# Retention attention with a routed mixture of experts on one core: the gate arithmetic moved away from in front of the token counts

## The chip, the cores and the metric

The kernel is one program on one core of a Trainium2 chip. The metric is the device time of one execution in microseconds, less is better. A profiled execution of the kernel before the change is shown beside its timed runs.

## The reference

A retention attention (a linear attention with a decay per head) over 4 sequences of 768 tokens with 8 heads of 64 gives a matrix `x` of 3072 tokens by 512. Each token then goes to one of eight experts, and its result is weighted by a gate:

```
state = gamma * state + k_t v_t^T ;  y_t = scale * q_t state
x = y laid out as (3072, 512)
logits = x @ w_gate ;  e_idx = argmax(logits) ;  probs = softmax(logits)
gate_w = probs[n, e_idx] ;  eom = 1 / (1 + exp(-(x @ w_output_gate)))
for e in 0..7:  rows of expert e:
    out = gate_w * eom[:, e] * (relu(x @ w1[e]) @ w2[e])
```

## The kernel before

The work has three stages.

**Attention.** The 3072 tokens are 24 chunks of 128, `i` from 0 to 23, and one pass of the loop does one chunk. The order of PE (TensorE), DVE (VectorE), ACT (ScalarE) and POOL (GpSimd) is the order in which the code is written. In a chunk PE makes the scores `s` (L331), starts the output `py` from the state (L348), transposes the next chunk's keys into `pk` and queries into `pq` (L286, L304), transposes finished rows of an earlier chunk into `px` (`tokens`, L453), adds the masked scores to `py` (L353), and updates the state `st` (L361). DVE masks the scores into `am` (L335) and scales `py` into `yt` (L369). ACT copies `pk` to `kt` (L288) and `px`, times the gate, to a `row` (L506). The tiles `pk`, `pq` and `px` take turns in two PSUM buffers (pool `ps_t`, tag `t`), so `px` takes the buffer that `pk` had, and it can start only when ACT has copied `pk` out.

**Routing, in pairs of chunks.** For pair `n`, the even chunk computes the logits in the PSUM tile `misc` (L379, `route1`), and at its end `route1b` and `out_gate`. The odd chunk that follows computes the gate and the place of each token:

- `gates` (L467, L468): sum of the exponentials and the small constant. `gates_b` (L475, L477): the product with the output gate's denominator, and the reciprocal `gate`.
- `count` (L460, L461): two small matmuls that count, per expert, the tokens ahead of each token. They write columns 0 to 15 of the same `misc` tile in which `gates` and `gates_b` read and write other columns, and they are ordered with every earlier access to that tile.
- `route2` (L484 to L496): the row number `posi` of each token in the sorted buffer `srt` in DRAM.
- `build_row` and `scatter` (L506, L513): the finished rows, sent to `srt` by an indirect DMA from POOL.

Chunk 11 also ranks the experts by the counts so far, and chunk 19 (`EARLY`) looks whether the first expert has 256 rows.

**The head.** The 256 first rows of the likeliest expert are loaded from `srt` at chunk 21 (L577), split into two parts on ACT and POOL in chunk 22 (`head_prep`, L590 to L594), and multiplied by that expert's weights. These 192 matmuls (L603, L621) are a generator, and `run_head(n)` issues the next `n` of them, to fill holes of PE: `HB` of them in chunk 23, `H1`, `H2` and `H3` in the routing of the last pair, 24 behind it, and the rest after a branch on `n_low` (L781, L782), the number of experts with few tokens, which every engine reads. Their results go out through eight indirect DMAs of 128 rows of 128 numbers (L185, `ot`, `idx`).

Behind the last counts `totals` (L547, L549, L550) computes the tokens per expert. The last two rows are scattered, and SP loads the sorted rows of the first expert as soon as these scatters have landed (L832, `xl`), then the weights of the second expert, then the second expert's rows.

**Experts.** Eight experts of 8 steps each: `stage1` (L867) gives `h`, ACT and DVE split it into `hh` and `hl` (L871, L872), `stage2` (L885) of a step needs both and is issued behind the next step's `stage1`. `prep_x` (L848 to L855: `idi`, `xt`, `xh`, `xw`) prepares the next expert's rows, and `split_weights` (L176 to L181) its weights. In this stage the order on ACT, DVE and SP is set by a scheduler, that on PE and POOL by the code.

Of the kernel before, what the change touches and what calls it, by code (L numbers as in the profile page):

```python
# [32 lines left out]
def retention_moe_kernel(  # L33
# [159 lines left out]
    with ExitStack() as actx:  # L193
# [118 lines left out]
        yts, rt = {}, {}  # L312
# [72 lines left out]
        def small(name, *shape, dt=F32, bufs=2):  # L385
            return sm.tile([P, *shape], dt, name=name, tag=name, bufs=bufs)
# [42 lines left out]
        def route1b(n):  # L429
            oh, _, wm, acc = rt["r", n]  # L430
            lg, wk = rt.pop(("l", n))
            zk = in_psum(n, 128, 2, E)
            nc.vector.tensor_tensor(out=zk, in0=lg[:, :, E:2 * E], in1=oh, op=ALU.mult)
            z = small("z", 2)
            nc.vector.tensor_reduce(out=z, in_=zk, axis=AX.X, op=ALU.add)
            rt["z", n] = z

            nxt = small("acc", 2, E, dt=BF16)
            nc.vector.scalar_tensor_tensor(out=nxt[:, 0], in0=wk[:, 1], scalar=wm[:, 1:2], in1=acc[:, 1],
                                           op0=ALU.is_equal, op1=ALU.add)  # L440
            rt["acc"] = nxt

        def out_gate(n):
            ez = small("ez", 2)
            nc.scalar.activation(ez, rt.pop(("z", n)), AF.Exp, scale=-1.0)
            rt["ez", n] = ez
# [9 lines left out]
        def count(n):  # L456

            oh, acc = rt["r", n][0], rt["r", n][3]
            cnt = rt["misc", n][:, 0:2 * E]
            nc.tensor.matmul(cnt, tri_b, oh.rearrange("p c e -> p (c e)"), start=True, stop=False)  # L460
            nc.tensor.matmul(cnt, ones_b, acc.rearrange("p c e -> p (c e)"), start=False, stop=True)  # L461

        def gates(n):
            _, ex, wm, _ = rt["r", n]

            se = in_psum(n, 160, 2)
            nc.vector.tensor_reduce(out=se, in_=ex, axis=AX.X, op=ALU.add)  # L467
            nc.vector.tensor_scalar(out=se, in0=se, scalar1=1e-9, scalar2=None, op0=ALU.add)  # L468
            rt["se", n] = se

        def gates_b(n):
            wm = rt["r", n][2]
            se, ez = rt.pop(("se", n)), rt.pop(("ez", n))
            den = in_psum(n, 162, 2)
            nc.vector.scalar_tensor_tensor(out=den, in0=ez, scalar=1.0, in1=se, op0=ALU.add, op1=ALU.mult)  # L475
            gate = small("gate", 2)
            nc.vector.reciprocal(gate, den)  # L477
            rt["gate", n] = (gate, wm)

        def route2(n):  # L480
            oh, _, wm, _ = rt.pop(("r", n))
            cnt = rt["misc", n][:, 0:2 * E].rearrange("p (c e) -> p c e", c=2)
            rk = in_psum(n, 164, 2, E)
            nc.vector.tensor_tensor(out=rk, in0=cnt, in1=oh, op=ALU.mult)  # L484
            rank = in_psum(n, 180, 2)
            nc.vector.tensor_reduce(out=rank, in_=rk, axis=AX.X, op=ALU.add)

            ok = in_psum(n, 182, 2, E)
            nc.vector.tensor_scalar(out=ok, in0=cnt, scalar1=float(SLOTS), scalar2=None, op0=ALU.max)
            ov = small("ov", 2)  # L490
            nc.vector.tensor_reduce(out=ov, in_=ok, axis=AX.X, op=ALU.add)
            slot = small("slot", 2)
            nc.vector.scalar_tensor_tensor(out=slot, in0=wm, scalar=-float(SLOTS), in1=rank, op0=ALU.mult, op1=ALU.add)
            nc.vector.scalar_tensor_tensor(out=rank, in0=rank, scalar=float(SLOTS), in1=ov, op0=ALU.is_ge, op1=ALU.mult)
            posi = small("posi", 2, dt=I32, bufs=5)
            nc.vector.scalar_tensor_tensor(out=posi, in0=slot, scalar=float(E * SLOTS), in1=rank, op0=ALU.add, op1=ALU.max)  # L496
            rt["posi", n] = posi
# [68 lines left out]
        EARLY = 8  # L566
        LOAD0 = 2 * EARLY + 5
        backlog = []
        HB, H1, H2, H3 = 12, 8, 5, 4


        hd = {}
# [67 lines left out]
        def run_head(n):  # L640
            for _ in range(n):
                next(head, None)
# [17 lines left out]
        for i in range(NCH):  # L660
            b, c = divmod(i, NC)
            if i == LOAD0:

                n_late = nc.values_load(late[0:1, 0:1], min_val=0, max_val=1)
                with tc.If(n_late > 0):
                    fill(base0, cnt0, 0, HEAD, sm)
                head_load()
            if i + 3 < NCH:
                load_k(i + 3)
                load_v(i + 3)  # L670
            if i % 2 == 0 and i // 2 + 3 < B * NQ:
                load_q(i // 2 + 3)
            if 1 <= i < NC:
                more_gq(i)
            for e in clear_at.get(i, ()):
                clear(e)
            if i in w_at:
                load_weights(w_at[i])
            if i + 2 < NCH:
                prep_v(i + 2)  # L680

            n1 = i // 2 - 1 if i % 2 == 0 else -1
            n2 = i // 2 - 1 if i % 2 == 1 else -1

            def between():
                if n1 >= 0:
                    logits(n1)
                if i + 1 < NCH:
                    kt_block(i + 1)
                if i == 1:  # L690
                    spread_gates()
                if 0 < i and i + 2 < NCH:
                    qt_block(i + 2)
                if i == NCH - 1:
                    run_head(HB)
                if n1 >= 0:
                    route1(n1)
                if n2 >= 0:
                    gates(n2)
                    gates_b(n2)  # L700
                    count(n2)
                    misc = rt["misc", n2]
                    if n2 == PICK:
                        rank(totals(misc, rt["acc"][:, 0]), io8, pick)
                        nc.vector.tensor_copy(base0, pick[:, 0:1])
                        nc.vector.tensor_scalar(out=first, in0=io8, scalar1=base0, scalar2=None, op0=ALU.is_equal)
                        nc.vector.tensor_scalar(out=base0, in0=base0, scalar1=float(SLOTS), scalar2=None, op0=ALU.mult)
                        rank_e[0] = nc.values_load(pick[0:1, 0:1], engines=(mybir.EngineType.SP,), min_val=0, max_val=E - 1)
                    if n2 == EARLY:
                        tot = totals(misc, rt["acc"][:, 0])  # L710
                        cj = sm.tile([P, E], F32, name="cj", tag="cj")
                        nc.vector.scalar_tensor_tensor(out=cj, in0=tot, scalar=1.0, in1=first, op0=ALU.mult, op1=ALU.mult,
                                                       accum_out=cnt0)
                        nc.vector.tensor_scalar(out=late, in0=cnt0, scalar1=float(HEAD), scalar2=None, op0=ALU.is_lt)
                if i >= 3:
                    tokens(i - 3)
                if i == NCH - 1:
                    tokens(i - 2)
            def before_state():
                if i == 0:  # L720
                    qr_block(2)
                    qt_block(2)
                if n2 >= 0:
                    route2(n2)
                if i >= 3:
                    build_row(i - 3)
                if i + 3 < NCH:
                    qr_block(i + 3)

            attend(i, between, before_state)  # L730
            if n1 >= 0:
                route1b(n1)
                out_gate(n1)
            if i == NCH - 1:
                build_row(i - 2)
                break
            if i == LOAD0 + 1:
                head_prep()
            if i == LOAD0 - 1:
                flush(len(backlog))  # L740
            elif i == LOAD0:
                flush(len(backlog))
            elif i >= first_scatter:
                flush(2)
            for z in range(2):
                if i - 2 - z in w_at:
                    split_weights(w_at[i - 2 - z] + z)
# [4 lines left out]
        n = NCH // 2 - 1  # L752
# [5 lines left out]
            tokens(2 * n + c2, pl[:, c2])  # L758
        run_head(H3)
        count(n)  # L760
        route1b(n)
        out_gate(n)
        gates(n)
        gates_b(n)
        tot = totals(rt["misc", n], rt["r", n][3][:, 1], rt["r", n][0][:, 1])
        route2(n)
        for c2 in range(2):
            build_row(2 * n + c2)
# [7 lines left out]
        for j, n in enumerate((FILL, FILL - P)):  # L776
            nc.vector.tensor_scalar(out=lw, in0=cnts, scalar1=float(n), scalar2=None, op0=ALU.is_lt)
            nc.vector.tensor_reduce(out=no, in_=lw, axis=AX.X, op=ALU.add)
            nc.vector.tensor_copy(n_low[:, j:j + 1], no)
        run_head(24)  # L780
        n_few = nc.values_load(n_low[0:1, 0:1], min_val=0, max_val=E)  # L781
        with tc.If(n_few > 0):  # L782
            for e in range(E):
# [311 lines left out]
```

## Time and profile before

| What | Value |
|---|---|
| Time of the kernel before, median of 3 runs | 462.39 us (461.76 to 464.07) |
| Profiled execution, its own time | 463.1 us |
| Profiled execution, its span | 461.4 us |
| PE matmul busy | 434.5 us (94%) |
| DVE busy | 252.0 us (55%) |
| ACT busy | 191.3 us (41%) |
| POOL busy | 185.8 us (40%) |
| Mean granted TensorE clock | 0.973 |

Busy time is the sum of an engine's instructions. Matmuls are pipelined, so a busy PE can still be slower than its best. The clock is a share of full speed. The attention takes the span's first 157 us or so, the head's matmuls fill PE up to about 180 us, and the rest are the experts.

### The profile page before, as it was taken

The numbers are of one execution on the slowest core, as the hardware profiler recorded it, in microseconds if no ns is written. First come the engines' busy times: TensorE is split into PE (matmuls) and PEld (weight loads), VectorE is DVE, ScalarE is ACT, GpSimd is POOL, SyncE is SP. The second block draws the span as 40 slices with busy tenths as digits, with TensorE's granted clock in tenths as the row PEclk, the third lists the DMA queues.
The fourth block names the chain that finished last, engine by engine and source line by source line (L and its number), as shares of the span: only waits on it lengthen the run. The fifth ranks groups of instructions, "written<-read, shape, count | busy, mean of one in ns | idle before, by whom it ended". The sixth has DMA issues, their size and how long they took to land.

```text
span 461.4 us, 9939 instructions
## 1 busy us (share of the span) xinstructions
PE 434.5 (94%) x3586; PEld 398.1 (86%) x3586; DVE 252.0 (55%) x673; ACT 191.3 (41%) x391; POOL 185.8 (40%) x242
## 2 busy tenths in 40 slices
PE   8999999999996799699999999999999999999993
PEld 5787777777775698699999999999999999999882
DVE  1356767766664516655465476375475476476101
ACT  3335554567753212454343353353353353453111
POOL 4433184558956212404102720720740740721702
PEclk9889999999998799999999999999999999999997
DMA  9968999999821139256823942953863852860102
GB/s 208 208 148 254 243 274 270 282 280 253 231 71 48 46 98 244 62 181 194 183 91 122 247 148 91 240 184 93 210 201 93 219 193 93 232 177 7 53 7 69
DMA packets 110068, 75.52 MB, mean 164 GB/s; under 512 B 55459, under 2 KB 97447, under 8 KB 110008
## 3 DMA queue, kind: packets, MB, share of 16 engines
q1 hardware_dynamic: 104720, 62.03, 52.3%
q0 software_dynamic: 5120, 12.69, 8.3%
q8 instruction: 30, 0.49, 0.5%
q14 instruction: 30, 0.25, 0.2%
q10 hardware_dynamic: 168, 0.06, 0.1%
HBM read 59.41 MB, written 15.83 MB: 163 GB/s over the span
## 4 chain that ended last, share of the span: by engine, by line
issue 43%; PE 28%; POOL 13%; DMA 6%; DVE 6%; ACT 2%; POOLq 0%; DVEq 0%; ACTq 0%
POOL out_dram L185 12%; PE py L353 5%; PE s L331 5%; DMA out_dram<-ot,idi 5%; PE h L603 3%; DVE am L335 3%; PE px L453 3%; PE a L621 2%; PE st L361 2%; PE pk L286 2%; PE misc L379 2%; ACT kt L288 1%; PE py L348 1%; PE pw L140 1%; DMA out_dram<-ot,idx 1%
## 5 line engine op out<-in xcount | busy, mean ns | idle before, releaser
L185 POOL DMA_INDIRECT out_dram<-ot,idi x84 | 87.7, 1044 | 160.6 <-DVE ot L891 137.1
L867 PE MATMUL h<-xh,whi 128*128 128x224 f32 (+7 forms) x256 | 86.5, 338 | 1.1 <-issue 1.1
L867 PE MATMUL h<-xw,whi 128*128 128x224 f32 (+7 forms) x256 | 86.3, 337 | 0.0
L867 PE MATMUL h<-xh,wlo 128*128 128x224 f32 (+7 forms) x256 | 86.2, 337 | 0.0
L885 PE MATMUL a<-hh,whi 128*128 128x224 f32 (+6 forms) x224 | 75.4, 337 | 2.5 <-ACT hh L871 2.5
L885 PE MATMUL a<-hl,whi 128*128 128x224 f32 (+6 forms) x224 | 75.8, 338 | 1.3 <-DVE hl L872 1.3
L885 PE MATMUL a<-hh,wlo 128*128 128x224 f32 (+6 forms) x224 | 75.5, 337 | 0.0
L180 DVE TENSOR_TENSOR wlo<-raw,whi 128x512 fp32r<-128x512 f32 x56 | 38.3, 683 | 58.3 <-ACT whi L176 53.7
L176 ACT CAST whi<-raw 128x512 fp32r<-128x512 f32 x64 | 39.7, 620 | 70.0 <-PE a L885 68.4
L871 ACT ACTIVATE hh<-h 128x224 fp32r<-128x224 f32 (+7 forms) x64 | 31.0, 485 | 87.8 <-PE h L867 82.8
L872 DVE SCALAR_TENSOR_TENSOR hl<-h,hh 128x224 fp32r<-128x224 f32 (+7 forms) x64 | 35.0, 546 | 58.8 <-ACT hh L871 58.8
L867 PEld LDWEIGHTS h<-xh,whi 128*128 128x128 f32 x256 | 48.6, 190 | 2.1 <-issue 1.2
L867 PEld LDWEIGHTS h<-xw,whi 128*128 128x128 f32 x256 | 48.6, 190 | 0.8
L867 PEld LDWEIGHTS h<-xh,wlo 128*128 128x128 f32 x256 | 48.5, 190 | 0.6
L885 PEld LDWEIGHTS a<-hh,whi 128*128 128x128 f32 x224 | 42.5, 190 | 3.2 <-ACT hh L871 2.7
L885 PEld LDWEIGHTS a<-hl,whi 128*128 128x128 f32 x224 | 42.6, 190 | 2.1 <-DVE hl L872 1.6
L885 PEld LDWEIGHTS a<-hh,wlo 128*128 128x128 f32 x224 | 42.6, 190 | 0.4
L513 POOL DMA_INDIRECT srt<-row,posi x24 | 24.4, 1018 | 40.8 <-ACT sd L365 13.2
L177 ACT CAST whi<-raw 128x512 fp32r<-128x512 f32 x64 | 39.4, 616 | 0.2 <-DMA raw<-in_moe_w_dram 0.2
L335 DVE TENSOR_TENSOR am<-s,mask 128x512 f32<-128x512 f32 x48 | 30.9, 685 | 14.1 <-PE s L331 13.5
L181 DVE TENSOR_TENSOR wlo<-raw,whi 128x512 fp32r<-128x512 f32 x56 | 38.3, 683 | 0.1
L281 POOL TENSOR_TENSOR vs<-vn,gv 128x512 f32<-128x512 f32 x24 | 25.1, 1046 | 30.4 <-PE st L361 14.2
(168 smaller groups left out, 675.4 us busy)
## 6 DMA issues: line engine op xcount, KB each, us to landing
raw<-in_moe_w_dram SPq DMA_DIRECT2D x32, 512.0 KB, 5.3
raw<-in_moe_w_dram SPq DMA_DIRECT2D x32, 256.0 KB, 5.0
raw<-in_moe_w_dram SPq DMA_DIRECT2D x64, 128.0 KB, 3.2
kn<-in_k_dram SPq DMA_DIRECT2D x24, 256.0 KB, 5.4
qn<-in_q_dram SPq DMA_DIRECT2D x12, 512.0 KB, 6.5
vn<-in_v_dram SPq DMA_DIRECT2D x24, 256.0 KB, 5.7
srt<-zrow SPq DMA_DIRECT2D x8, 325.0 KB, 5.2
xl<-srt SPq DMA_DIRECT2D x12, 211.2 KB, 6.3
```

Of the source, the lines that this page charges most:

```text
L176: nc.scalar.copy(cols(hi), r1)
L177: nc.scalar.copy(perm(hi), r2)
L180: eng.tensor_sub(cols(lo), r1, cols(hi).bitcast(F32))
L181: eng.tensor_sub(perm(lo), r2, perm(hi).bitcast(F32))
L185: st = nc.gpsimd.indirect_dma_start(out=dst, out_offset=bass.IndirectOffsetOnAxis(ap=idx, axis=0), in_=src, in_offset=None, bounds_check=n ...
L281: nc.gpsimd.tensor_mul(vs[i], vn.pop(i), gv[:, c, :].unsqueeze(2).broadcast_to([P, H, D]))
L335: nc.vector.tensor_tensor(out=a, in0=pss[hh], in1=mask.unsqueeze(1).broadcast_to([P, NG, P]), op=ALU.mult)
L513: st = nc.gpsimd.indirect_dma_start(out=srt, out_offset=bass.IndirectOffsetOnAxis(ap=posi, axis=0), in_=row, in_offset=None, bounds_check= ...
L867: nc.tensor.matmul(ps[:, 0:C], l[:, 0, w], r[:, dc, 0:C], start=(n == 0), stop=(n == 3 * NDC - 1))
L871: nc.scalar.activation(hh, ps[:, 0:C], AF.Relu)
L872: nc.vector.scalar_tensor_tensor(out=hl, in0=ps[:, 0:C], scalar=0.0, in1=hh.bitcast(F32), op0=ALU.max, op1=ALU.subtract)
L885: nc.tensor.matmul(accs[d][:, 0:C], l[:, 1, w], r, start=(f == 0 and n == 0), stop=(f == NF - 1 and n == 2))
```

## The change

`gates` of a pair moves from the odd chunk to the end of the even chunk before it, behind `route1b` and `out_gate`. `gates_b` moves from in front of `count` to the place right in front of `route2`. In the last pair, `totals` moves from behind `gates_b` to directly behind `count`. `H3` goes from 4 to 12 head matmuls, and the share of the head that is issued ahead of the branch from 24 to 40.

```diff
-        HB, H1, H2, H3 = 12, 8, 5, 4
+        HB, H1, H2, H3 = 12, 8, 5, 12
...
                 if n2 >= 0:
-                    gates(n2)
-                    gates_b(n2)
                     count(n2)
                     misc = rt["misc", n2]
...
                 if n2 >= 0:
+                    gates_b(n2)
                     route2(n2)
...
             if n1 >= 0:
                 route1b(n1)
                 out_gate(n1)
+                gates(n1)
...
         run_head(H3)
         count(n)
+        tot = totals(rt["misc", n], rt["r", n][3][:, 1], rt["r", n][0][:, 1])
         route1b(n)
         out_gate(n)
         gates(n)
         gates_b(n)
-        tot = totals(rt["misc", n], rt["r", n][3][:, 1], rt["r", n][0][:, 1])
         route2(n)
...
-        run_head(24)
+        run_head(40)
```

On DVE, from the end of chunk 4 into chunk 5 (`am` is the masked score of chunk 5, `misc` the routing tile of the pair that is being counted), the difference reads:

```order
 L439 SCALAR_TENSOR_TENSOR acc<-misc,wm,acc 128x8
-L335 TENSOR_TENSOR am_683<-s_673,mask 128x512
-L335 TENSOR_TENSOR am_685<-s_674,mask 128x512
-L467 TENSOR_REDUCE misc<-misc 128x2
-L468 TENSOR_SCALAR misc<-misc 128x2
+L467 TENSOR_REDUCE misc<-misc 128x2
+L468 TENSOR_SCALAR misc<-misc 128x2
+L335 TENSOR_TENSOR am_685<-s_675,mask 128x512
+L335 TENSOR_TENSOR am_687<-s_676,mask 128x512
 L475 SCALAR_TENSOR_TENSOR misc<-ez,misc 128x2
 L477 RECIPROCAL gate<-misc 128x2
```

The two instructions of `gates` now stand ahead of the two masks. L475 and L477 keep their place on DVE, but they are now written behind `count`, so they wait for its matmuls and no longer the matmuls for them.

On PE in the last pair, the rows from the transposes' end to the counts before the change (`a` and `h` are the head's):

```order
L621 MATMUL a_2623<-h_2597,whi 128x256
L621 MATMUL a_2623<-h_2597,wlo 128x256
L621 MATMUL a_2623<-h_2597,whi 128x256 x2
L460 LDWEIGHTS tri_b
L460 MATMUL misc<-oh,tri_b 128x16
L461 LDWEIGHTS ones_b
L461 MATMUL misc<-acc,ones_b 128x16
L547 LDWEIGHTS ones_b
L547 MATMUL misc<-acc,ones_b 128x8
```

The same place on PE after the change:

```order
L621 MATMUL a_2623<-h_2597,whi 128x256
L621 MATMUL a_2623<-h_2597,wlo 128x256
L621 MATMUL a_2623<-h_2597,whi 128x256 x2
L621 MATMUL a_2623<-h_2597,wlo 128x256
L621 MATMUL a_2624<-h_2597,whi 128x256 x2
L621 MATMUL a_2624<-h_2597,wlo 128x256
L621 MATMUL a_2624<-h_2597,whi 128x256 x2
L621 MATMUL a_2624<-h_2597,wlo 128x256
L603 MATMUL h_2659<-xh_2496,whi 128x256
L460 LDWEIGHTS tri_b
L460 MATMUL misc<-oh,tri_b 128x16
```

Eight more head matmuls stand ahead of the counts. The counts and the totals follow each other on PE in both, but before the change L547 was written behind `gates_b`. On DVE, L550, which copies the totals, moves from behind L477 to ahead of L433, the first instruction of `route1b`.

The scheduler of the last stage also gives another order on ACT and DVE at one place, when the second expert's rows arrive. On DVE both first `hl` now stand ahead of `idi`, and the split of one weight step stands between the parts of `prep_x`:

```order
-L872 SCALAR_TENSOR_TENSOR hl<-h,hh 128x224
+L872 SCALAR_TENSOR_TENSOR hl<-h,hh 128x224 x2
 L848 CAST idi<-xl 128x14
-L872 SCALAR_TENSOR_TENSOR hl<-h,hh 128x224
+L853 STREAM_TRANSPOSE xt<-xl 128x448 x2
+L855 TENSOR_TENSOR xw<-xt,xh 128x448
+L180 TENSOR_TENSOR wlo<-raw,whi 128x512
+L181 TENSOR_TENSOR wlo<-raw,whi 128x4x4x32
+L855 TENSOR_TENSOR xw<-xt,xh 128x448
 L853 STREAM_TRANSPOSE xt<-xl 128x448 x2
 L855 TENSOR_TENSOR xw<-xt,xh 128x448 x2
```

What moved there is an `hl`, to ahead of the wait for the rows; the third `hl` stands behind all four `xw` in both kernels.

## Rows read from the trace of the kernel before

**Rows 1.** Windows by stage: busy us (instructions) per engine, PEclk, DMA share, GB/s.

```profile
40.00:138.00 98.00, 92.47 (x1386) 74.98 (x1387) 67.68 (x257) 58.23 (x129) 57.89 (x83) 1.00 0.92 243
176.00:186.50 10.50, 9.45 (x81) 9.09 (x80) 4.55 (x23) 1.10 (x3) 4.43 (x5) 1.00 1.10 246
193.94:197.20 3.26, 3.26 (x18) 3.26 (x17) 1.84 (x5) 1.14 (x2) 0.00 (x0) 0.50 0.27 91
194.00:461.40 267.40, 260.16 (x1437) 252.77 (x1436) 139.85 (x255) 103.09 (x194) 90.62 (x87) 0.99 0.51 144
```

**Rows 2.** Waits of PE in the whole span: total us, times, longest.

```profile
PE misc L460 <- DVE gate L477: 4.1, 10, 0.6
PE h L603 <- POOL xw L592: 2.7, 2, 2.0
PE a L885 <- ACT hh L871: 2.5, 1, 2.5
PE misc L547 <- DVE gate L477: 1.6, 1, 1.6
PE misc L460 <- ACT misc L425: 1.0, 1, 1.0
PE misc L379 <- DVE yt L369: 0.6, 1, 0.6
```

**Rows 3.** Timeline of chunk 17: start us, us, instruction [idle before <-releaser].

```profile
108.41 1.29 DVE L335 TENSOR_TENSOR am<-s,mask 128x512 f32<-128x512 f32 x2 [0.41 <-PE s L331]
109.76 0.59 ACT L288 COPY kt<-pk 128x512 f32<-128x512 f32 x1 [0.22 <-PE pk L286]
110.58 0.64 PE L453 MATMUL px<-ident,yt 128*128 128x128 f32 x4
```

**Rows 4.** Timeline of chunk 16, all engines.

```profile
104.51 0.59 ACT L288 COPY kt<-pk 128x512 f32<-128x512 f32 x1 [0.24 <-PE pk L286]
105.15 0.66 PE L453 MATMUL px<-ident,yt 128*128 128x128 f32 x4
```

**Rows 5.** Timeline of chunks 3 and 21, first and last of ten.

```profile
33.35 0.59 ACT L288 COPY kt<-pk 128x512 f32<-128x512 f32 x1 [1.24 <-PE pk L286]
34.12 0.64 PE L453 MATMUL px<-ident,yt 128*128 128x128 f32 x4
...
130.99 0.59 ACT L288 COPY kt<-pk 128x512 f32<-128x512 f32 x1 [0.21 <-PE pk L286]
132.07 0.64 PE L453 MATMUL px<-ident,yt 128*128 128x128 f32 x4
```

**Rows 6.** Timelines of POOL and SP around the head rows.

```profile
134.01 1.95 SPq L577 DMA_DIRECT2D xl<-srt  x4
...
140.18 1.03 POOL L513 DMA_INDIRECT srt<-row,posi  x1 [4.75 <-DVE acc L439]
143.97 2.47 POOL L592 TENSOR_TENSOR xw<-xt,xh 128x512 fp32r<-128x512 f32 x2
```

**Rows 7.** Timeline behind the last counts.

```profile
158.50 0.17 DVE L477 RECIPROCAL gate<-misc 128x2 f32<-128x2 f32 x1
159.15 0.18 DVE L484 TENSOR_TENSOR misc<-misc,oh 128x16 f32<-128x16 f32 x1
161.19 0.98 POOL L513 DMA_INDIRECT srt<-row,posi  x1 [4.42 <-DVE lw L777]
```

**Rows 8.** Timeline from the sorted rows' load to the next expert.

```profile
166.87 3.20 SPq L832 DMA_DIRECT2D xl<-srt  x4
...
180.84 0.98 POOL L185 DMA_INDIRECT out_dram<-ot,idx  x1 [17.41 <-DVE no L793]
182.13 0.97 POOL L185 DMA_INDIRECT out_dram<-ot,idx  x1 [0.30 <-issue]
...
186.75 0.18 DVE L848 CAST idi<-xl 128x14 int32<-128x14 f32 x1 [3.56 <-DMA xl<-srt]
...
193.03 0.38 DVE L872 SCALAR_TENSOR_TENSOR hl<-h,hh 128x224 fp32r<-128x224 f32 x1
```

## The prediction, made before the change was run

> **What bounds the kernel now.** I read the busy time by stage first, then the list of what PE waited for, then the timeline around each of those waits, and last the chain from the last counts to the experts. The windows show PE busy 92.5 of 98 us in the attention and 260 of 267 us in the experts, at a granted clock of 1.00 and 0.99 [rows 1]: wherever PE is not held up, it is the bound. So only its waits can give time back, and the list of them is short [rows 2]. Two entries are what the change takes away: ten waits of the counts for the reciprocal, 4.1 us together, and one wait of the totals for the last reciprocal, 1.6 us. A third, 1.0 us, is the hole ahead of the last counts, where PE has run out of head matmuls. The reader should see that the sum, 6.7 us or 1.4% of the time, is only a ceiling. Each of these waits has another one close behind it, and what the change is worth depends on how close.
>
> **Attention, the ten waits.** In an odd chunk the order on PE is: queries' transposes, counts, `px`, `py`. The counts waited for `gates_b`, which sat behind the masks on DVE. Without it they can run as soon as the transposes are done. But `px` takes the PSUM buffer of `pk`, so it must wait for ACT's copy `kt`. An even chunk, which has no counts, shows how close that bound is: `kt` ends at 104.51 + 0.59 = 105.10, and `px` starts at 105.15 [rows 4], 0.05 us behind it. In chunk 17 `kt` ends at 110.35, so `px` could start at 110.40, and it does at 110.58 [rows 3]: the gain is 0.18 us, although PE's wait there was about 0.4. In the first of the ten, chunk 3, it is 34.12 - (33.35 + 0.59 + 0.05) = 0.13 us, in the last, chunk 21, 132.07 - (130.99 + 0.59 + 0.05) = 0.44 us [rows 5]. Read in the same way, chunks 5 to 19 give 0.28, 0.28, 0.21, 0.21, 0.17, 0.18, 0.18 and 0.20. Together the ten are 2.28 us, not 4.1.
>
> Two of them don't arrive. In chunk 11 DVE ranks the experts between the counts and `yt`, and the next logits wait 0.6 us for `yt` [rows 2]. In the changed order the ranking starts earlier, but L475 and L477 then stand between it and `route2`, so `yt` comes about when it did: 0 instead of 0.21. The 0.44 of chunk 21 lies behind the head's load, which is issued at 134.01 from rows scattered in chunk 20. POOL's scatter of chunk 21's row stands still until 140.18, with 4.75 us idle in front of it, and I take it to wait for that load to land, since it writes the buffer that the load reads (the profile names a DVE instruction that ended just before). Behind it come `xw` at 143.97 [rows 6] and PE's 2.7 us of waiting for `xw` [rows 2]. That chain moves with chunk 20, not with chunk 21. So chunks 3 to 9 (0.90) and 13 to 19 (0.73) remain: **1.63 us**.
>
> What the move costs DVE: L467 and L468 are about 0.2 us each and now stand ahead of the masks, where DVE sat idle for 0.41 us until the scores came [rows 3]. They fit into that hole. Where they didn't, the masks would be late by up to 0.4 us, but `py`, which reads them, follows 0.6 us behind `px`, so they still end at 109.70 or a little later against a `py` at about 111. In chunk 22 they delay the head's transposes by 0.4 us; POOL, which is behind, covers that. L475 now waits for the counts and holds `route2` behind it, but the counts come earlier by what `gates_b` took, so `posi` and `yt` stay where they were. I cost all of this at nothing; the bounds are 0 and 0.05 us for each of ten chunks.
>
> **The last pair.** Here the chain is: counts, `gates_b`, `route2`, scatter, load of the sorted rows by SP, the second expert's weights and rows on the same queue, and their arrival. L484, the first of `route2`, started at 159.15, behind totals that waited for L477, which started at 158.50 [rows 7]. In the new order L550 goes ahead of `route1b` and pushes everything by one slot of about 0.21 us, and L484 follows L477 by another: 158.50 + 0.21 + 0.21 = 158.92. So `posi` and the scatter at 161.19 are earlier by **0.23 us**. With twelve head matmuls in front, the counts themselves are no earlier: they wait for ACT's exponentials, the 1.0 us entry of the list.
>
> PE, though, gets its two holes filled, 2.6 us, so the head ends up to 2.6 us earlier. **I cost this gain at zero**, because PE doesn't lie on the chain that comes next. The sorted rows' load goes out at 166.87, the second expert's rows arrive at 186.75, and the `hl` that PE needs stands behind all of their preparation on DVE, at 193.03 [rows 8]; on ACT the `hh` in front of it makes PE wait 2.5 us [rows 2]. None of these waits for the head. A PE that comes earlier waits longer at the same `stage2`. The new order around `idi` saves the second `hl`, but the third still stands behind the same four `xw`, so it changes nothing either. If that cover were gone, the 2.6 us would count. The larger share ahead of the branch (40) is there so that PE doesn't reach the branch before `n_low` is known; a wait there, up to 1 us, would be hidden by the same chain.
>
> **What a faster head triggers.** Its eight output DMAs start at 180.84 and follow each other by 1.29 us [rows 8], and the second expert's rows are under way then. In the window in which this happens the DMA engines are fully taken (share 1.10) and move 246 GB/s [rows 1]. If the outputs start about 2.4 us earlier, two more of them get in front of the arrival: 2 x 128 x 128 x 4 bytes are 131 kB, 0.53 us at that rate. The bounds are 0 (they find gaps) and 2.6 us (each holds the engines for its whole slot). I take **0.53 us**, since the window's rate is that of the same mixture of transfers. [...]
>
> **The sum.** -1.63 - 0.23 + 0.53 = -1.33 us against the profiled execution's 463.1, so 461.8. That execution is 0.7 above the median of the runs shown, 462.39, so the median becomes **461.1 us**. 0.5% is 2.3 us, about what a measurement of this kernel can tell from no change.
>
> **The clock.** [...] I leave it as it is and keep plus and minus 1.6 us for the range. [...]
>
> **The rivals.**
>
> - *All of it arrives.* The holes of PE are closed and nothing else takes their place: 463.1 - 6.7 = 456.4, by the median 455.7. For it speaks that PE is the bound nearly everywhere; against it the 0.05 us between `kt` and `px`, and the arrival at 186.75, which doesn't depend on PE. Chance 0.11.
> - *The slow stretch goes away.* PE's work resumes at full clock: 1.6 us less than the forecast, 459.5 by the median. [...] Chance 0.13.
> - *The outputs get in the way of the second expert's rows.* One mechanism, at the arrival at 186.75: at 2.6 us instead of 0.53 the result is 0.7 us slower than before, 463.1 by the median. It decides from 1.86 us on, where it eats the whole gain, and only from 4.2 us on would it be measurable. For it speaks the share of 1.10; against it the small size, 131 kB. Chance 0.14.
> - *The change does nothing.* The scatter's wait in chunk 21 is not for the load but for something fixed, or `gates` delays the masks after all, so that the attention's gain is gone: 462.4. Chance 0.07.
> - *The forecast*, 461.1 with a range of its own of 460.0 to 462.2: chance 0.55.
>
> Faster by over 0.5% (below 460.1) are the first rival, the second, and a part of the forecast's own spread, 0.08: 0.32. Slower by over 0.5% (above 464.7) is the far end of the third, with a longer slow stretch: 0.06. The rest, 0.62, is within. The range reaches down past the second rival, to 458.8, and up to the third, 463.2; the first and the far end of the third stay out.
>
> **What would show it.** Right: the counts no longer wait for L477, and `px` waits for `kt` in odd chunks as it does in even ones, so that the source of ten waits changes rather than disappears. The scatter behind the last counts is earlier by some 1.9 us, the head's end by some 4, and the wait of PE ahead of the third `stage2` is longer by 2 us or more. Wrong: PE's first `hl` of the second expert's preparation much earlier than 2 us, which would mean that the arrival at 186.75 depends on the head; a shift in the attention near 4 us, so that `px` isn't bound by `kt`; or a span that differs by the length of slow-clock stretches elsewhere.

## The result, and the profile after the change

The changed kernel takes 460.07 us (median of 13 runs, 457.59 to 461.41), the kernel before 462.37 (13 runs beside them). The ratio is 0.9942 with a 95% interval of 0.992 to 0.9964, so 1.7 to 3.7 us faster. Here and below, a ratio leaves out executions more than 1.5% above the shortest of their kernel (slow ones), and the profiles of `e3_xfirst_after`, `e8_tail_again` and `e12_both` were taken in such executions. The profiled execution took 460.33 us with a span of 458.6 at a mean clock of 0.973; before it was 463.1 and 461.4 at the same clock.

PE's waits after the change, in the same view as [rows 2] (total us, times, longest):

```profile
PE a L885 <- ACT hh L871: 5.6, 1, 5.6
PE h L603 <- POOL xw L592: 2.2, 2, 1.8
PE px L453 <- ACT kt L288: 2.0, 10, 0.2
PE h L603 <- ACT xh L591: 1.6, 1, 1.6
...
PE a L621 <- DVE h L608: 0.7, 1, 0.7
PE misc L379 <- DVE yt L369: 0.6, 1, 0.6
```

The ten waits of the counts for `gate` (4.1 us) are gone, and ten waits of `px` for `kt` stand in their place, 2.0 us. The wait of the totals and the hole ahead of the last counts are gone too; a new wait of 0.7 us for DVE (`h`, L608) stands in the head behind the counts. What PE waits for `hh` ahead of the third `stage2` has grown from 2.5 to 5.6 us.

Chunk 17 in the timeline after the change, to be read against [rows 3]:

```profile
109.18 0.59 ACT L288 COPY kt<-pk 128x512 f32<-128x512 f32 x1 [0.21 <-PE pk L286]
109.44 0.17 PE L461 MATMUL misc<-acc,ones_b 128*128 128x16 bf16 x1
109.82 0.66 PE L453 MATMUL px<-ident,yt 128*128 128x128 f32 x4 [0.20 <-ACT kt L288]
```

The counts end at 109.61, and `px` starts at 109.82, 0.05 us behind the end of `kt` (109.18 + 0.59 = 109.77). That is the distance that even chunks had before the change [rows 4].

The last pair and the way to the second expert, to be read against [rows 7] and [rows 8]:

```profile
155.60 0.17 DVE L550 COPY cnts<-misc 128x8 f32<-128x8 f32 x1 [0.68 <-PE misc L549]
...
157.06 0.17 DVE L477 RECIPROCAL gate<-misc 128x2 f32<-128x2 f32 x1
157.27 0.18 DVE L484 TENSOR_TENSOR misc<-misc,oh 128x16 f32<-128x16 f32 x1
159.30 0.98 POOL L513 DMA_INDIRECT srt<-row,posi  x1 [4.22 <-DVE top L558]
165.00 1.97 SPq L832 DMA_DIRECT2D xl<-srt  x4
176.21 0.97 POOL L185 DMA_INDIRECT out_dram<-ot,idx  x1 [14.65 <-DVE no L793]
184.31 0.17 DVE L848 CAST idi<-xl 128x14 int32<-128x14 f32 x1 [4.44 <-DMA xl<-srt]
190.03 0.56 PE L885 MATMUL a<-hh,whi 128*128 128x224 f32 x1 [5.61 <-ACT hh L871]
190.30 0.38 DVE L872 SCALAR_TENSOR_TENSOR hl<-h,hh 128x224 fp32r<-128x224 f32 x1
```

The scatter is 1.89 us earlier, the head's first output 4.63 (180.84 to 176.21), but the second expert's rows only 2.44 (186.75 to 184.31) and `hl` 2.73 (193.03 to 190.30). The head's earlier end is spent in PE's wait.

**Where the 2.8 us between the two spans lie.** From the `kt` of chunk 4 (33.35 before, 34.01 after) to the head's first matmul (142.12 and 141.30) it is 108.77 against 107.29 us: -1.48. From there to the last counts (156.94 and 155.26) it is 14.82 against 13.96: -0.86. From the counts to the ninth `stage2` (213.34 and 210.86) it is 56.40 against 55.60: -0.80. The start of the attention was 0.66 us later, and -0.3 comes behind the ninth `stage2`.

The scatter's 1.89 us add up from the later start (+0.66), the first two stretches (-1.48 and -0.86) and the last pair (-0.21). The forecast's 1.9 was 1.63 and 0.23, so that the two agree is in part luck.

The -0.86 is not an effect of the change that any run shows. By PE's rows, 0.68 of it are the eight head matmuls behind `py` of chunk 23 (150.99 to 152.97 before, 149.97 to 151.27 after), which ran at the low clock before (0.52 in that stretch, 0.86 after), and 0.20 are a shorter wait for `xw`. From the last transposes (154.45 and 152.76) to the counts it is 2.49 and 2.50 us: the eight added matmuls fill the hole, and the counts come no earlier. The windows from 142 to 154 us (busy us and count per engine, PEclk, DMA share, GB/s), before:

```profile
142.00:146.00 4.00, 1.68 (x10) 1.30 (x10) 1.18 (x5) 0.05 (x1) 4.00 (x6) 1.00 0.11 43
146.00:150.00 4.00, 3.51 (x22) 3.08 (x24) 1.08 (x7) 1.45 (x3) 2.28 (x8) 0.51 0.19 71
150.00:154.00 4.00, 4.00 (x30) 3.06 (x29) 1.02 (x2) 0.53 (x2) 2.00 (x3) 0.64 0.34 133
```

And after:

```profile
142.00:146.00 4.00, 1.81 (x9) 1.28 (x7) 0.00 (x0) 0.00 (x0) 3.84 (x7) 0.69 0.00 0
146.00:150.00 4.00, 4.00 (x29) 3.28 (x27) 1.42 (x9) 1.65 (x3) 2.26 (x6) 0.50 0.19 71
150.00:154.00 4.00, 4.00 (x37) 3.46 (x36) 1.85 (x6) 0.76 (x2) 1.18 (x2) 0.96 0.34 133
```

The clock is low for as long in both: what is missing to 1.00 adds up to 0.85 windows of 4 us (0.49 + 0.36 before, 0.31 + 0.50 + 0.04 after), which at a clock of 0.50 is 6.8 us. After the change it falls earlier, while PE waits for the head's rows anyway, and so costs less. In five other runs of code without the filled holes, the distance from the head's first matmul to the counts is 12.98, 13.88, 14.00, 14.05 and 14.13 us, and in seven other runs with them 13.84 to 14.56. So the filled holes don't shorten it, and the 14.82 of the profiled kernel before is on the long side.

### The profile page after: what moved, and what is told of

Its sections match the earlier page's. It is cut to its first block, busy times and chain, and to the rows that moved or that the text cites. A ratio compares the mean times of both kernels' runs of the same rounds, so it can differ in the third digit from the quotient of the medians.

```text
span 458.6 us, 9941 instructions
## 1 busy us (share of the span) xinstructions
PE 433.8 (95%) x3586; PEld 397.5 (87%) x3586; DVE 252.7 (55%) x673; ACT 191.2 (42%) x391; POOL 185.6 (40%) x242
## 4 chain that ended last, share of the span: by engine, by line
issue 44%; POOL 12%; DMA 4%; PE 3%; DVE 0%; POOLq 0%
POOL out_dram L185 12%; DMA out_dram<-ot,idi 3%; PE a L621 2%; PE h L603 1%; DMA out_dram<-ot,idx 1%; DVE ot L633 0%; POOLq L185 0%; DVE no L793 0%; DVE tj L792 0%; POOLq L967 0%
```

## The experiments

The chips of the experiments ran the kernel before in 498 to 502 us instead of 462, so totals are compared only with runs beside them, and small effects are read from marks in the traces ahead of 220 us. What is longer there lies in the experts: from 200 us on, ACT stands still five to seven times for up to 10 us, for something that the profile calls remote and that the traces of before and after do not have.

**One part at a time.** The gate's move alone (`e1_att`, first diff) and the tail alone (`e2_tail`, second), each against the kernel before:

```diff
-                    gates(n2)
-                    gates_b(n2)
                     count(n2)
...
+                    gates_b(n2)
                     route2(n2)
...
                 out_gate(n1)
+                gates(n1)
```

```diff
-        HB, H1, H2, H3 = 12, 8, 5, 4
+        HB, H1, H2, H3 = 12, 8, 5, 12
...
         count(n)
+        tot = totals(rt["misc", n], rt["r", n][3][:, 1], rt["r", n][0][:, 1])
...
-        tot = totals(rt["misc", n], rt["r", n][3][:, 1], rt["r", n][0][:, 1])
...
-        run_head(24)
+        run_head(40)
```

> The kernel before with only the gate's move in the attention: the sum and the small constant at the end of the even chunk, product and reciprocal behind the counts. The last pair, its totals and the head's shares stay as before. My theory, that the gain comes from the ten odd chunks and is cut off by kt: 1.6 us faster than before, with px 0.05 us behind kt in the odd chunks and no wait of the counts left there. Rival, the tail (totals and filled holes) makes the gain: within 0.5 us of before. Rival, all of the ten waits arrive: 4.1 us faster.

> The kernel before with only the tail's part: totals directly behind the last counts, 12 head matmuls in front of them, 40 ahead of the branch; the attention's gates as before. My theory, that the head's holes are hidden behind the second expert's rows: 0.2 us faster at most, 0.3 slower at worst, although the head ends some 2.5 us earlier, and the wait of PE ahead of the third stage2 becomes longer by as much. Rival, the closed holes count: 1.0 to 2.6 us faster, with the wait no longer than before.

Each was run a second time, on another chip:

> Once more the kernel before with only the gate's move in the attention, since the weights of the experts arrived late in the run before. My theory 1.6 us faster than before; the head's end no earlier than by this. Rival (the tail makes the gain) within 0.5 us of before.

> Once more the kernel before with only the tail's part, for the same reason. My theory between 0.2 us faster and 0.3 us slower than before, with the last scatter 0.2 us earlier behind the counts and the head's end 2.6 to 3 us earlier. Rival (the closed holes count) 1.0 to 2.6 us faster.

The totals don't decide. Against the kernel before, the gate's move alone gave 1.0044 (1.0004 to 1.0084) and then 0.9968 (0.9929 to 1.0006), the tail alone 1.0084 (1.0034 to 1.0134) and then 0.9997 (0.9959 to 1.0034). By the medians of all runs it is 1.0008 and 0.9976 for the gate's move, 0.9982 and 1.0032 for the tail. Which part looks better changes from chip to chip, by as much as the effect. The marks do decide. In the attention, the distance from one `kt` to the next holds the `px` of the odd chunk before (us, read from the starts of `kt`):

| `px` of chunk | 3 | 5 | 7 | 9 | 11 | 13 | 15 | 17 | 19 | 21 |
|---|---|---|---|---|---|---|---|---|---|---|
| gain reckoned from `kt` | 0.13 | 0.28 | 0.28 | 0.21 | 0.21 | 0.17 | 0.18 | 0.18 | 0.20 | 0.44 |
| before | 5.83 | 4.92 | 5.98 | 5.91 | 5.48 | 5.87 | 5.88 | 4.82 | 5.91 | 6.15 |
| after | 5.72 | 4.66 | 5.72 | 5.72 | 5.36 | 5.72 | 5.73 | 4.65 | 5.72 | 5.72 |
| `e2_tail` | 5.83 | 4.92 | 6.13 | 5.72 | 5.43 | 5.82 | 5.80 | 4.66 | 5.72 | 6.04 |
| `e1_att` | 5.72 | 4.66 | 6.47 | 5.72 | 5.31 | 5.72 | 5.72 | 4.66 | 5.72 | 5.72 |

Before minus after is 2.03 us for the ten. Chunk 7 is disturbed in all runs on these chips; without it, it is 1.77 us, and before minus `e1_att` is 1.82. `e2_tail` has none in chunks 3 and 5 (5.83 and 4.92, as before) and 6.04 against 5.72 in chunk 21. In chunks 9, 17 and 19 it is as short as after the change, but its ten waits for `gate` are all still there (4.3 us); the even chunk before is 0.2 to 1.3 us longer there than in the profiled kernel before, so that these three distances decide nothing. The list of waits does: `e1_att` has none of the counts for `gate` left, and nine of `px` for `kt`. So the attention's gain is the gate's move, and it has the size that the end of `kt` sets.

Behind the last counts (all times are distances from the last L460; three kernels without the tail's part, four with it):

| From the last counts to | without: before, `e1_att`, `e7_att_again` | with: after, `e2_tail`, `e8_tail_again`, `e11_state_first` |
|---|---|---|
| scatter | 4.25, 4.25, 4.25 | 4.04, 4.05, 4.04, 4.04 |
| head's end (`ot`) | 22.15, 22.14, 22.03 | 19.20, 19.20, 19.20, 19.19 |
| issue of the second expert's rows | 20.22, 19.43, 19.44 | 18.81, 18.82, 18.80, 18.80 |
| their arrival (`idi`) | 29.81, 29.46, 29.12 | 29.05, 29.35, 30.99, 27.86 |
| third `stage2` | 35.65, 35.80, 36.04 | 34.77, 35.06, 36.69, 35.47 |
| ninth `stage2` | 56.40, 56.02, 57.86 | 55.60, 55.70, 57.98, 56.16 |

Two rows of `e2_tail` show the cover at work, the head's end at 176.79 and the third `stage2` at 192.65, behind a wait:

```profile
176.79 1.48 DVE L633 STREAM_TRANSPOSE ot<-a 128x256 f32<-128x256 f32 x4 [0.68 <-PE a L621]
...
192.65 0.55 PE L885 MATMUL a<-hh,whi 128*128 128x224 f32 x1 [3.76 <-ACT hh L871]
```

The head ends 2.9 us earlier behind the counts in every kernel with the tail's part. At the second `stage2` all of it is still there (29.16 to 29.29 without, 26.31 to 26.35 with). At the third the means are 35.83 and 35.50, at the ninth 56.76 and 56.36; without `e8_tail_again`, 35.10 and 55.82. So 0.3 to 0.9 us are left, with a spread of 0.4 to 2.4 us between runs of the same tail. The theory holds for the holes: they are lost between the second and the third `stage2`.

The 2.9 us are not the two holes alone. The wait of the totals gave 1.6 us and the eight matmuls moved ahead 0.9. Behind that wait the clock was low, and no longer is. Before the change and after it:

```profile
159.00:163.00 4.00, 4.00 (x23) 4.00 (x23) 2.69 (x20) 1.41 (x3) 1.51 (x2) 0.59 0.08 29
```

```profile
157.00:161.00 4.00, 3.30 (x29) 3.10 (x27) 3.37 (x22) 1.92 (x4) 1.40 (x2) 1.00 0.04 17
```

In the six traces without the tail's part the clock is 0.50 for 3.4 us, from 1.4 to 2.8 us behind the last counts on; in the eight with it, it stays at 1.00 up to the head's end. In the kernel before these are 17 head matmuls at 0.21 us and not 0.12, some 1.5 us. The new wait for DVE and smaller holes take about 1.2 us back.

**The second expert's rows first.** A first attempt to take the cover away:

```diff
+            if s == 0:
+                load_x(1)
             while loaded < min(NS, s + NF + 1):
                 load_weights(loaded)
...
-            if f == 2 and e + 1 < E:
+            if f == 2 and 0 < e < E - 1:
```

> The changed kernel, with the load of the second expert's rows issued ahead of the two weight loads that stood before it on SP's queue (5.7 us earlier there). My theory, that this arrival is what hides the head's end: the rows arrive 4 to 6 us earlier, PE's 5.6 us of waiting ahead of the third stage2 shrink below 1 us, and the time is 4 to 6 us below the changed kernel. Rival, the DMA engines are the bound and the weights are late by as much instead: within 1 us of the changed kernel, with a wait for raw or whi in the place of this one.

> The kernel before with the same edit, the second expert's rows loaded ahead of the two weight loads. PE waited 3.8 us there for hh and hl, so my theory gives 3 to 4 us less than before, and with the cover gone the change is worth 4 to 5 us between this run and the one of the changed kernel with the same edit: 1.6 from the attention, 0.2 from the last pair and the 2.6 of the holes that were costed at nothing. Rival, the holes are worth nothing for another reason: 1.6 to 2.7 us between the two.

495.91 us beside 498.13 (no interval) for the changed kernel, 1.0049 (0.9998 to 1.0101) for the kernel before. The rows do arrive 6 us earlier behind the counts (22.90 instead of 29.05), but the third `hl` hardly (34.22 instead of 35.04). The timeline of ACT and DVE in `e3_xfirst_after` shows what took their place:

```profile
180.03 0.30 DVE L848 CAST idi<-xl 128x14 int32<-128x14 f32 x1
...
189.48 0.62 ACT L176 CAST whi<-raw 128x512 fp32r<-128x512 f32 x1 [4.67 <-remote]
190.14 0.69 DVE L180 TENSOR_TENSOR wlo<-raw,whi 128x512 fp32r<-128x512 f32 x1 [4.63 <-ACT whi L176]
191.35 0.38 DVE L872 SCALAR_TENSOR_TENSOR hl<-h,hh 128x224 fp32r<-128x224 f32 x1
```

`whi`, the second expert's first weight step, stands ahead of the third `hh` in ACT's order and is 4.67 us late, and `wlo` ahead of `hl` on DVE. The rival was right in that another wait takes the place of this one. That the weights landed late is not shown: the releaser is given as remote, and the DMA engines' share is already down to 0.11 from 185 to 187 us. What was wrong in my theory is that the arrival alone is the cover. It is the order: the scheduler puts the second expert's preparation, which nobody needs until the ninth step, between the second and the third `hl`.

**The cover taken away by order.** First the rows alone are put behind the fourth `hl` (`e5_order_after`, `e6_order_before`):

```diff
+        def behind(e, i):
+            if e == 1:
+                tc.add_manual_dep(i.ins, hls[0].name, mybir.DependencyInfo(
+                    mybir.DependencyClass.Sync, mybir.DependencyReason.DATA), reason="behind the fourth hl")
...
-                nc.vector.tensor_copy(idi[:, 0:nb], t[:, 0:nb, P])
+                behind(e, nc.vector.tensor_copy(idi[:, 0:nb], t[:, 0:nb, P]))
```

> The changed kernel with one more rule of order for the scheduler: idi and the xt of the second expert come behind the fourth hl on DVE, so that hh and hl of the third and fourth step no longer stand behind rows that have not landed. My theory, that only this preparation hides the head's end: PE's 5.6 us of waiting ahead of the third stage2 shrink below 1 us, and with them the slow-clock stretch of 3 us behind the wait; 5 to 7 us less than the changed kernel, 455 us or less where that takes 460. Rival, the weights or another wait are due at the same time: less than 2 us.

> The kernel before with the same rule of order. PE waited 3.8 us there for hh and hl, so 3.8 to 5.4 us less than before. Between this run and the one of the changed kernel with the rule, my theory gives 4.2 to 4.7 us, since with the cover gone the head's earlier end (176.15 instead of 180.81) arrives in full. Rival, the closed holes are worth nothing for another reason: 1.5 to 2.8 us between the two, as without the rule.

0.9918 (0.9879 to 0.9957) and 0.9986 (0.9951 to 1.0022) against the kernel before. Then the first weight steps too (`e9_cover_after`, `e10_cover_before`): half of the rows behind the fourth `hl` and half behind the fifth, the splits emitted from the fourth step on.

```diff
-        nc.scalar.copy(cols(hi), r1)
-        nc.scalar.copy(perm(hi), r2)
+        for i in (nc.scalar.copy(cols(hi), r1), nc.scalar.copy(perm(hi), r2)):
+            if NF <= s < NF + 4:
+                tc.add_manual_dep(i.ins, hls[3 + (s - NF) // 2].name, mybir.DependencyInfo(
+                    mybir.DependencyClass.Sync, mybir.DependencyReason.DATA), reason="behind hl")
...
-            while split < min(NS, s + NF):
+            while s >= 3 and split < min(NS, s + NF) - (s == 3):
```

> The changed kernel with the cover taken away on both sides: on ACT and DVE the rows and the first four weight steps of the second expert are prepared behind the fourth hl and not between the second and the third, so that hh and hl of the third and fourth step wait neither for rows nor for weights that have not landed. My theory: PE reaches the third stage2 without the wait of 5.6 us and waits at most 1 us ahead of the fifth; 4 to 7 us less than the changed kernel, so 7 to 10 us less than before. Rival, the transfers of this stretch bound PE anyway, one step later: within 2 us of the changed kernel.

> The kernel before with the same edit. My theory: 2.5 to 5 us less than before, and 4.2 to 4.7 us more than the changed kernel with this edit, since without the cover the head's earlier end counts in full. Rival: the transfers bound PE in both, and the two differ by 2.7 us or less, as without the edit.

0.9916 (0.9881 to 0.995) and 0.9997 (0.9964 to 1.0031). Neither gain has the size that I expected: 4.1 and 4.2 us less than before instead of 7 to 10 for the changed kernel (0.82% of 501.75 and 0.84% of 501.22), 0.7 and 0.2 instead of 2.5 to 5.4 for the kernel before. ACT of `e9_cover_after` shows why:

```profile
178.26 0.36 ACT L878 ACTIVATE hh<-h 128x224 fp32r<-128x224 f32 x1 [4.97 <-DVE on L807]
182.47 0.36 ACT L878 ACTIVATE hh<-h 128x224 fp32r<-128x224 f32 x1 [3.85 <-PE h L874]
188.26 0.36 ACT L878 ACTIVATE hh<-h 128x224 fp32r<-128x224 f32 x1 [5.44 <-remote]
```

The second and third `hh` have nothing of the second expert ahead of them any more and are still late, the third by 5.44 us, with the releaser again given as remote. The kernel before with the same edit has such a stall of 6.15 us at the third `hh`. So the wait that I took away was followed by another. But the question that the pair was made for has its answer, since the stall is in both:

| From the last counts to | `e6_order_before`, `e10_cover_before` | `e5_order_after`, `e9_cover_after`, `e12_both` |
|---|---|---|
| head's end (`ot`) | 22.05, 21.95 | 19.19, 19.20, 19.19 |
| third `stage2` | 35.83, 35.63 | 33.09, 32.91, 32.92 |
| ninth `stage2` | 57.26, 57.37 | 54.33, 54.14, 53.84 |

With the preparation out of the way, the 2.8 us by which the head ends earlier are there at the third `stage2` (35.73 against 32.97), and 3.2 at the ninth. With it in the way, 0.3 to 0.9 were left. In totals the pairs differ by 0.0068 and 0.0081, 3.4 and 4.1 us, where the theory gave 4.2 to 4.7 and the rival 2.8 or less. By the intervals of the ratios each difference is uncertain by about 2.5 us, so the totals exclude neither; the marks decide.

**Is `kt` what holds `px`?** Half of the state's matmuls, which wait for nothing here, are put in front of `px`:

```diff
-            between()
+            between(state0)
...
+                state0()
                 if i >= 3:
                     tokens(i - 3)
```

(`state0` issues the matmuls of L361 for the first half of `g`, and the rest stay behind `py`.)

> The changed kernel with half of the state's matmuls (four of eight, some 0.3 us) in front of px and the other half where all were. My theory, that px is now held up by kt alone: the 0.2 us of PE's waiting ahead of px go in the seven odd chunks that update the state and stay in those that end a sequence; 1.4 us less than the changed kernel, and each such chunk 0.15 to 0.2 us shorter from kt to kt. Rival, py or yt comes later by the matmuls that went ahead and the next chunk waits for it: no change or slower by up to 3 us.

0.9952 (0.9917 to 0.9988) against the kernel before; on that chip the changed kernel itself wasn't run, so the totals say nothing of the 1.4 us. The distances from `kt` to `kt` do: for the `px` of chunks 3, 9, 13, 15, 19 and 21 they are 5.60, 5.48, 5.50, 5.50, 5.48 and 5.50, where the changed kernel has 5.72, 5.72, 5.72, 5.73, 5.72 and 5.72: 1.27 us in six chunks, 0.12 to 0.24 each. In chunks 5 and 17, which end a sequence and have no state matmuls, it is 4.66 and 4.66, against 4.66 and 4.65. Chunk 19 of that run in the timeline:

```profile
119.07 0.17 PE L470 MATMUL misc<-acc,ones_b 128*128 128x16 bf16 x1
...
119.19 0.45 PE L356 MATMUL st<-vs,kn 128*64 128x64 f32 x8
119.28 0.59 ACT L288 COPY kt<-pk 128x512 f32<-128x512 f32 x1 [0.69 <-PE misc L556]
119.92 0.66 PE L462 MATMUL px<-ident,yt 128*128 128x128 f32 x4 [0.28 <-ACT kt L288]
```

`px` starts where `kt` allows it, 119.28 + 0.59 + 0.05 = 119.92, and the state's half is done by then. So in an odd chunk `kt` is what stands in front of `px`, and work that is put in that place is free.

**Both edits.**

> The two edits on the changed kernel together, cover taken away and half of the state's matmuls first. They lie in different stages, so my theory adds them: 5 to 8 us less than the changed kernel, 8 to 11 less than before. Rival, only one of the two arrives.

0.9924 (0.9889 to 0.9958). The two don't add up beyond the 0.9916 of `e9_cover_after` on the same chip, though each shows in its own stage (the distances of the attention are those of `e11_state_first`, the ninth `stage2` comes 53.84 us behind the counts). In the profiled executions 3.4 us are lost behind the ninth `stage2` (290.8 us to the end against 287.4), where the stalls are; why the medians don't add up is not shown. `e5_order_after`, `e9_cover_after`, `e11_state_first` and `e12_both` are faster than the kernel before on their chips; that one of them beats the changed kernel was not timed side by side.

## Why the prediction was nearly right

The forecast was 461.1 us, 1.3 less than before; measured were 460.07, 2.3 less by the medians, at the lower edge of the forecast's own 460.0 to 462.2. By steps:

- **Attention, -1.63.** Right, and by the stated mechanism: 1.48 us to the head's first matmul. The ten waits for `gate` turned into ten for `kt`, as forecast. Chunk by chunk the gain is within 0.03 us of what the rows gave, with one exception: chunk 11, costed at 0, gave 0.12 of its 0.21, though the logits' wait for `yt` is 0.6 us as before. The 0.43 of chunk 21 was lost as forecast: the load at 134.01 moved to 133.10, the scatter still stood until 139.14, and PE's waits ahead of the head's matmuls add up to 3.8 us (2.2 and 1.6) as before (2.7 and 1.1).
- **Last pair, -0.23.** Right: the scatter is 0.21 us earlier behind the counts, in each of four kernels with the tail's part.
- **Closed holes, 0.** Right: the head ends 2.9 us earlier, and 0.3 to 0.9 us of all that the tail does reach the ninth `stage2`. That 2.9 is near the 2.6 of the two holes is luck: the slow stretch behind the totals' wait went too, which the forecast didn't see, and a new wait for DVE took most of that back. The reason given for the zero was right in kind and wrong in one detail. The cover is less the arrival of the rows than the place that the scheduler gives to their preparation and to the first weight steps, between `hl` of the second and the third step.
- **Outputs in front of the rows, +0.53.** No run bears this term out. From the issue of the second expert's rows to `idi` it takes 9.59, 10.03 and 9.68 us without the tail's part and 10.24, 10.53, 12.19 and 9.06 with it. The mean is 0.7 us longer, but the spread is 3 us, and without the 12.19 of `e8_tail_again` it is 0.2; so a delay of this size is neither shown nor excluded. That the outputs, issued by POOL, get in front of the rows, issued by SP, was my estimate from the share of 1.10 and the 246 GB/s of one window [rows 1]; no run here shows it.
- **What was missing, -0.4.** From the first expert's rows to the next weights' issue on SP it is 3.66 to 3.78 us in four runs without the tail's part (4.58 in the profiled kernel before, whose issue alone took 3.20 instead of 1.97) and 3.35 to 3.37 in those with it. With the scatter's 0.21 the second expert's rows are issued 0.6 us earlier behind the counts. In each trace without the tail's part, one of the four issues of the first expert's rows takes 0.6 to 1.6 us; in those with it all four take 0.3. Why is open: what SP waits for is not in its rows. By the marks, then, the tail gave 0.3 to 0.9 us where the forecast had it cost 0.3, and the attention 1.5 where it had 1.6. That makes 1.8 to 2.4 of the measured 2.3, but the interval of 1.7 to 3.7 us is wider than the 1.0 between forecast and result.
- **Clock, 0 plus or minus 1.6.** Right in its bounds. The 1.6 us is an estimate, half of the 3.26 us at 0.50 before the change [rows 1]; no run shows the term, and what the two profiles show in its place is 0.08 us (20.83 against 20.75, below). Behind the longer wait the slow stretch is longer: the clock is 0.50 for 6.8 us, from 187.9 to 194.7, where it was 3.4 us, from 193.8 to 197.3 [rows 1]. Windows of 4 us after the change:

```profile
186.00:190.00 4.00, 0.00 (x0) 0.00 (x0) 3.90 (x8) 2.52 (x7) 0.14 (x1) 0.74 0.05 16
190.00:194.00 4.00, 3.82 (x16) 3.55 (x17) 2.28 (x6) 2.01 (x5) 0.00 (x0) 0.50 0.20 62
194.00:198.00 4.00, 4.00 (x35) 4.00 (x35) 2.22 (x5) 1.89 (x4) 0.00 (x0) 0.91 0.69 200
```

  The clock falls at 187.9 while PE stands idle up to 190.03, so 2.1 us of the stretch cost nothing, and from the third to the ninth `stage2` it is 20.83 us instead of 20.75. What makes it fall there is not shown. The prediction named a span that differs by slow stretches elsewhere as a sign of being wrong, and two of them do differ: the one behind the last counts is gone, which is hidden like the rest of the head's earlier end, and the one between 142 and 154 us begins at another time, which no run ties to the change.

## What to carry to other kernels

A wait that is taken away is worth the distance to the next one at the same instruction, and a neighbouring iteration that never had the first wait shows that distance before anything is run. PE's holes count only if PE is what the next stage waits for; here the head ended 2.9 us earlier and 2.0 to 2.6 of it came back as a wait, because ACT and DVE had been given later work ahead of the operands that PE needed (after the change `hh` starts on ACT at 189.62 behind two `xh` from 188.63 on, and `hl` on DVE at 190.30 behind two `xw` from 189.22 on). Move that work behind, and the same edit is worth 2.8 to 3.2 us at that point.

## What the runs showed of the hardware

- On three chips, ACT stood still five to seven times in the experts, up to 10 us each and 32 to 47 us in all, about as much as the 36 to 40 us by which these runs are longer; PE and DVE stopped behind it. The profile calls the releaser remote. In `e9_cover_after`, the waits of `hh` on ACT from 200 us on:

```profile
ACT hh L878 <- remote: 31.3, 4, 9.0
```

  and one of them, with the end of the `stage1` that it needs:

```profile
256.99 0.35 PE L874 MATMUL h<-xh,wlo 128*128 128x416 f32 x1
...
264.68 0.52 ACT L878 ACTIVATE hh<-h 128x416 fp32r<-128x416 f32 x1 [8.65 <-remote]
```

  `h` was done at 257.34 and PE stood idle from 261.90 on, but `hh` began at 264.68, so ACT did not wait for work of PE. The cause is open. The two DMA queues that the profile marks as instruction (q8 and q14) carried the same in the traces of before and after as in eight of these runs: 30 packets each, 0.49 and 0.25 MB.
- The slow stretch between 142 and 154 us has the same length in both profiles, 6.8 us, but it begins 3.9 us behind the head's first matmul before and 2.2 after, and that alone moves the time by about 0.7 us (eight matmuls in 1.98 or 1.30 us).
- A wait of PE can cost more than its length: behind the holes of 1.0 and 1.6 us around the last counts the clock was 0.50 for 3.4 us in all six traces that have them, and in none of the eight that don't.
